# A hand-written issue order of 1,091 steps, listed anew, with one activation-table request ahead of the first logarithm

## The chip, the cores and the metric

The kernel runs on one NeuronCore of a Trainium2 chip. The core has five engines that work at the same time, each through its own instruction queue in order: TensorE (PE in the profile: matmuls; PEld: loads of the stationary operand), VectorE (DVE), ScalarE (ACT), GpSimd (POOL) and SyncE (SP, which here only issues DMAs). The metric is the device time of one execution in microseconds (us): the median of several runs.

## The reference, cut to what matters

```python
def _attn_ref(q, k, v, alpha):           # each (4, 8, 768, 48): batch, heads, tokens, head size
    state = zeros((B, H, 48, 48))
    for t in range(768):
        state = alpha[:, :, t, :, None] * state + einsum('bhd,bhe->bhde', k[:, :, t], v[:, :, t])
        y[:, :, t] = einsum('bhd,bhde->bhe', q[:, :, t], state)
    return y

x = y.transpose(0, 2, 1, 3).reshape(3072, 384)
h = x @ w_in                              # (384, 2048)
r = maximum(h, 0.0)
out = (s * (r * r) + b) @ w_out           # (2048, 384); s, b single numbers
```

A gated linear recurrence over 768 tokens gives 3072 rows of 384 numbers, which go through a two-layer network with a squared ReLU. Inputs and output are 32-bit floats.

## The kernel before, in words

**Blocks.** The 3072 rows are cut into 24 blocks of 128 rows, numbered n (or g) from 0 to 23; six blocks make one batch entry, and the state starts anew at blocks 0, 6, 12 and 18. Blocks 0 to 5, called windowed, are handled in pairs: an even block holds heads 0 to 3 and the following odd one heads 4 to 7 of the same 256 tokens.

**The recurrence of a block**, by the names of the steps and with the engine of each:

- `ln n` (ScalarE, L214): logarithm of alpha into la. `cum n` (TensorE, L225, L228, L239): running sums of it by matmuls with a triangle of ones, into the accumulator bank ct_ps.
- `ex n` (ScalarE, L249, L250, L253): exponentials of the sums and of their negatives, bi and b. For a windowed block a third gives the decay of the block (blast). For other blocks `decay n` (SyncE, L263, L265) writes the last row of b to DRAM and reads it back transposed, in three DMAs.
- `km n` and `qm n` (VectorE, L271, L279): k times bi, q times b. `tr n 1` and `tr n 0` (TensorE, L292): their transposes, again into ct_ps. `cp n` (VectorE, L299): copy of both out of ct_ps.
- `amat n` (TensorE, L320): products of k and q, into the two a_ps banks. `am n` (VectorE, L325): two masked copies out of them.
- `vcast n` (GpSimd, L219): v to 16 bits.
- `yi n` (TensorE, L340): the part of y from the state of the block before. `ya n` (TensorE, L356, L366): the part from within the block.
- `sp n` (TensorE, L382, L391): the block's addition to the state. `t1 n` (VectorE, L434, L436): new state. `sd n` and `sc n` (GpSimd, L444, L450): the state times the decay, for the next block's yi and t1.
- `yev n` (ScalarE, L400), `xt n` (TensorE, L408), `xev n` (ScalarE, L420): y out of its bank, transposed, and to 16 bits: the input of the network.

**The network of a block**, in four quarters u: `mp g u` (TensorE, L475, 12 matmuls of 128x128) into one of two banks h_ps in turn, `rl g u` (ScalarE, L489) the ReLU, `sq g u` (VectorE, L496) the square, `o g u` (TensorE, L511, 4 matmuls with 384 columns) into o_ps, and `oev g` out of it: by ScalarE (L524) for the first 13 blocks, which are kept and get their bias later (`add_bias`, VectorE, L563), by VectorE with the bias (L528) for the others. `store n` (SyncE) writes the rows. The last block's output is done in two halves of the columns (L539, L548).

**Setup.** `load_w` loads a pair of windowed blocks, whole or four heads at a time, `load` one block, `load_w_in i` and `load_w_out j0 j1` quarters of the weights (768 KB each). `win i kk` casts a piece of w_in to 16 bits (`a`: ScalarE, L619, `v`: VectorE, L621), `wout` a piece of w_out times s (VectorE, L171, or ScalarE, L179). `spread` (TensorE, L199, then VectorE) brings s and b to all partitions. `colsum`, `bias_sum` (VectorE, L186 to L191) and `bias_row` (TensorE, L195) form the bias row. `zero`, `ones`, `upper`, `eye` and `masks` fill constants on VectorE and GpSimd. `busy 1` is a matmul of 128x512 (L204) whose result nobody reads: filler work on TensorE; there are 37 of them. `table` (L569) requests, on ScalarE, the activation table that holds both logarithm and exponential; where an activation is met whose function is not in the table loaded last, the compiler puts a load of another table ahead of it.

**What sets the order.** No scheduler reorders anything. The string `order` (L629) lists 1,091 steps; the loop at L711 calls them one after the other, and each appends its instructions to the queues of its engines. So the list is, engine by engine, the order of each queue; waits between engines are put in from the data each step reads and writes. SyncE's queue is in list order too: a DMA whose buffer is not yet free, or a decay row not yet computed, holds every later DMA. DMAs take eight completion counters in turn, and one more is issued only when the eighth before it has landed.

## Time and profile before

| | |
|---|---|
| median of 3 runs | 199.38 us (199.14 to 199.48) |
| the profiled execution | 198.8 us, of which the profile's span is 197.0 us |
| TensorE busy | 186.6 us, 95% of the span |
| VectorE busy | 147.7 us, 75% |
| ScalarE busy | 119.6 us, 61% |
| GpSimd busy | 67.1 us, 34% |
| DMA | 30.34 MB moved; share of the 16 DMA engines about 1.0 up to 47 us, 0.55 from 47 to 191 us |
| first matmul, first `mp`, last matmul group | 1.94 us, 22.78 us, 191.16 us |

The span is one profiled execution on the chip, from its first to its last instruction. Busy time of TensorE counts a matmul until its modelled end, and matmuls overlap: the mean duration of an `mp` matmul is 219 ns, while one starts every 56 ns. To see a delay of TensorE, one compares the starts of successive matmuls. A row of the timeline gives start, duration, engine, line of the kernel, operation, result and operands, shape, and in brackets the idle time of the engine ahead of it with what ended it. A row of the waits gives who waited, for whom, the total, how often, and the longest.

### The profile page before, as it was taken

What the parts mean: (1) busy time and instruction counts of PE and PEld (TensorE: products, weight loads), DVE (VectorE), ACT (ScalarE), POOL (GpSimd) and SP (SyncE); (2) the same over time, 40 slices, a digit from 0 to 9 for tenths busy, and PEclk for the clock granted to TensorE, in tenths of its full rate; (3) what the DMA queues carried; (4) which work ended last, traced back from release to release, by engine and by line L of the source; (5) the groups of instructions that cost most, each with busy time, mean ns of one, the idle gap of its engine ahead of it and who ended that gap; (6) DMA issues with size and microseconds to landing.
All of it is one profiled execution on the core that took longest, in us unless ns stands there. A gap on an engine that the chain in (4) does not pass through costs nothing.

```text
span 197.0 us, 6345 instructions
## 1 busy us (share of the span) xinstructions
PE 186.6 (95%) x2593; PEld 146.6 (74%) x2595; DVE 147.7 (75%) x303; ACT 119.6 (61%) x246; POOL 67.1 (34%) x98
## 2 busy tenths in 40 slices
PE   4898999999999999999899899999999999999993
PEld 1466789757798877887577787887887778788873
DVE  5457897888689799588458476878988898885551
ACT  3825778934677849585437667657567465673530
...
GB/s 152 313 342 364 322 373 352 195 187 209 87 4 2 162 219 28 122 173 153 1 149 141 115 43 164 1 10 178 138 172 112 138 91 176 6 230 134 203 120 80
DMA packets 101119, 30.34 MB, mean 154 GB/s; under 512 B 94291, under 2 KB 99554, under 8 KB 101090
## 3 DMA queue, kind: packets, MB, share of 16 engines
...
q8 instruction: 20, 0.33, 0.7%
...
## 4 chain that ended last, share of the span: by engine, by line
PE 79%; DVE 8%; POOL 3%; ACT 3%; DMA 3%; issue 2%; POOLq 0%; ACTq 0%; DVEq 0%
PE h_ps L475 29%; PE o_ps L511 25%; PE ct_ps L292 5%; PE a_ps L320 4%; DMA a_sb<-in_alpha_dram 3%; PE o_ps L204 3%; POOL sd_sb L444 3%; DVE gt_all L496 2%; PE y_ps L366 2%; PE h_ps L408 2%; PE a_ps L539 1%; PE y_ps L340 1%; PE ct_ps L225 1%; PE p_ps L391 1%; DVE kb_sb L271 1%
## 5 line engine op out<-in xcount | busy, mean ns | idle before, releaser
L489 ACT ACTIVATE r_sb<-h_ps 128x512 bf16<-128x512 f32 x94 | 55.6, 599 | 33.7 <-PE h_ps L475 28.8
L475 PE MATMUL h_ps<-xd_all,w_in_bf 128*128 128x128 bf16 x1128 | 75.0, 219 | 0.0
L475 PEld LDWEIGHTS <-w_in_bf 128*128 128x128 bf16 x1152 | 67.7, 98 | 4.2
L511 PE MATMUL o_ps<-w_out_bf,gt_all 128*128 128x384 bf16 x336 | 64.7, 326 | 0.0
L444 POOL TENSOR_TENSOR sd_sb<-t_sb,blast_all 48x192 bf16<-48x192 f32 x40 | 29.3, 732 | 72.4 <-DVE t_sb L436 34.9
L511 PEld LDWEIGHTS <-gt_all 128*128 128x128 bf16 x368 | 32.8, 98 | 17.0 <-DVE gt_all L496 0.9
L496 DVE TENSOR_TENSOR gt_all<-r_sb 128x512 bf16<-128x512 bf16 x96 | 41.4, 456 | 5.2 <-ACT r_sb L489 5.2
L450 POOL TENSOR_TENSOR sc_sb<-t_sb,blast_all 112x384 f32<-112x384 f32 x16 | 17.6, 1100 | 29.0 <-DVE t_sb L436 15.9
L299 DVE COPY qkT<-ct_ps 112x1024 bf16<-112x1024 bf16 x24 | 16.5, 687 | 12.2 <-PE ct_ps L292 9.5
L219 POOL CAST v_bf<-v_sb 128x384 bf16<-128x384 f32 x24 | 17.6, 752 | 12.5 <-DMA v_sb<-in_v_dram 10.0
L271 DVE TENSOR_TENSOR kb_sb<-k_sb,bi_sb 128x384 bf16<-128x384 f32 x24 | 14.4, 600 | 7.3 <-ACT bi_sb L249 7.3
L249 ACT ACTIVATE bi_sb<-ct_ps 128x384 f32<-128x384 f32 x24 | 11.8, 490 | 12.3 <-PE ct_ps L225 6.2
L279 DVE TENSOR_TENSOR qb_sb<-q_sb,b_sb 128x384 bf16<-128x384 f32 x24 | 14.2, 591 | 5.0 <-ACT b_sb L250 4.9
L325 DVE TENSOR_TENSOR am_a<-a_ps,mask 128x512 bf16<-128x512 f32 x18 | 12.3, 684 | 5.6 <-PE a_ps L320 5.6
L420 ACT ACTIVATE xd_all<-h_ps 128x384 bf16<-128x384 bf16 x24 | 11.8, 490 | 5.4 <-PE h_ps L408 5.2
L400 ACT ACTIVATE y_bf<-y_ps 128x384 bf16<-128x384 f32 x21 | 10.4, 493 | 6.7 <-PE y_ps L366 5.5
L204 PE MATMUL o_ps<-mask,U_bf 128*128 128x512 bf16 x35 | 11.5, 456 | 2.3 <-DVE mask L600 1.9
L214 ACT ACTIVATE la_sb<-a_sb 128x384 bf16<-128x384 f32 x24 | 12.4, 519 | 0.0
L325 DVE TENSOR_TENSOR am_b<-a_ps,mask 128x512 bf16<-128x512 f32 x18 | 12.2, 678 | 0.0
L250 ACT ACTIVATE b_sb<-ct_ps 128x384 f32<-128x384 f32 x24 | 11.8, 492 | 0.0
L292 PE MATMUL ct_ps<-ident,kb_sb 128*112 128x128 bf16 x96 | 9.8, 225 | 0.8 <-DVE kb_sb L271 0.8
L292 PE MATMUL ct_ps<-ident,qb_sb 128*112 128x128 bf16 x96 | 9.8, 225 | 0.1
...
## 6 DMA issues: line engine op xcount, KB each, us to landing
...
```

The lines of the kernel that those rows point to most:

```text
L204: nc.tensor.matmul(out=o_ps, lhsT=U_bf, rhs=mask4.rearrange("a p t -> a (p t)"), start=True, stop=True,)
L219: nc.gpsimd.tensor_copy(out=by_head(v_bf[n % 3], n), in_=by_token(rows("v", n), n))
L271: nc.vector.tensor_tensor(out=by_head(kb_sb[n % 3][:, :, 0:48], n), in0=by_token(rows("k", n), n), in1=by_head(bi_sb[n % 2], n), op=ALU.mult,)
L292: nc.tensor.transpose(out=o, in_=t.rearrange("a h d -> a (h d)")[:, 128 * p : 128 * p + 112], identity=ident,)
L299: nc.vector.tensor_copy(out=qkT_sb[n % 2][0:112].rearrange("a x p t -> a (x p t)"), in_=t_ps[0:112].rearrange("a x p t -> a (x p t)"),)
L325: nc.vector.tensor_tensor(out=am_sb[e][n % 2], in0=a_ps[e], in1=m, op=ALU.mult)
L444: nc.gpsimd.tensor_tensor(out=sd_sb[n % 2][r, :, d], in0=t1_sb[r, :, d], in1=bl[r].to_broadcast([48, NP, 48]), op=ALU.mult)
L450: nc.gpsimd.tensor_tensor(out=sc_sb[0:112], in0=t1_sb[0:112], in1=blast[n % 4][0:112].to_broadcast([112, NP, 96]), op=ALU.mult,)
L475: nc.tensor.matmul(out=hp[:, jj * N : (jj + 1) * N], lhsT=w_in_bf[:, kk, 128 * j : 128 * (j + 1)], rhs=xd_sb[g][:, kk, 0:N], start=(kk == ...
L489: nc.scalar.activation(out=rs, in_=h_of.pop((g, u)), func=AF.Relu)
L496: nc.vector.tensor_tensor(out=gt_sb[g][:, u * 512 : (u + 1) * 512], in0=rs, in1=rs, op=ALU.mult)
L511: nc.tensor.matmul(out=op[:, 0:d_model], lhsT=gt_sb[g][:, j * C : (j + 1) * C], rhs=w_out_bf[:, j, :], start=(j == 0), stop=(j == NJ - 1),)
```

## The change

Both kernels call the same steps with the same arguments, only in another order; two things belong to it.

- `table` stands ahead of `ln 1; ln 0`, the first two logarithms. Before, it stood behind `ex 0`. The first logarithm is now ln 1, then ln 0.
- All of the list is written anew: filler matmuls, constants, loads, casts and the steps of the blocks stand in other places. For instance `spread` comes behind `tr 0 0`, `zero sd` and `win 2 2 v` come between `am 0` and `cp 1`, the first network quarter is `mp 0 0` instead of `mp 0 1`, `colsum 1` and `colsum 2` come behind `qm 5`, and `vcast 11` comes ahead of `sd 10`.

The diff, cut to the beginning of both lists and to the places that the prediction speaks of:

```diff
-        zero blast; zero ones_g; load_w a 0 0 4; upper n; load_w a 0 4 8; load_w k 0 0 4; zero kb; masks n; busy 1; ones g;
-        load_w q 0 0 4; load_w a 1; zero qb; busy 1; zero la; load_w q 0 4 8; busy 1; upper w; busy 1; zero sd; busy 1;
-        load_w k 0 4 8; load_w q 1; scalars; ln 0; load_w v 0; ln 1; cum 0; load_w_in 1; ex 0; table; busy 1; eye; ones f;
-        busy 1; busy 1; km 0; qm 0; tr 0 1; tr 0 0; masks w; busy 1; busy 1; busy 1; cp 0; cum 1; ex 1; load_w k 1; busy 1;
-        amat 0; busy 1; busy 1; km 1; busy 1; load_w_in 2; qm 1; busy 1; busy 1; ln 2; vcast 0; load_w_in 0; busy 1; am 0;
-        tr 1 1; tr 1 0; busy 1; busy 1; busy 1; cp 1; busy 1; spread; amat 1; am 1; cum 2; ex 2; busy 1; busy 1; busy 1;
-        ya 0; vcast 1; load_w v 1; sp 0; sp 1; ya 1; busy 1; busy 1; busy 1; busy 1; busy 1; win 1 0 a; yev 0; xt 0;
-        load_w a 2; ln 3; qm 2; xev 0; t1 0; km 2; tr 2 1; tr 2 0; load_w_in 3; sd 0; win 1 1 v; yi 1; win 1 2 v; busy 1;
-        cp 2; busy 1; load_w k 2; busy 1; busy 1; sc 0; win 2 1 v; yev 1; win 2 2 v; t1 1; win 2 0 a; busy 1;
-        load_w_out 0 4; win 0 2 v; cum 3; busy 1; busy 1; xt 1; ex 3; vcast 2; xev 1; km 3; amat 2; win 0 1 v; qm 3; am 2;
-        win 0 0 a; mp 0 1; load_w q 2; mp 1 2; rl 0 1; rl 1 2; load_w_out 4 8; tr 3 1; tr 3 0; mp 0 0; rl 0 0; sc 1; sd 1;
...
-        wout 2 4 0; sq 2 0; rl 2 1; t1 3; wout 0 2 1; mp 0 3; yi 3; yev 3; load_w v 2; mp 2 2; sc 3; load k 6; sq 1 3;
-        mp 2 3; o 2 0; rl 2 2; qm 4; tr 4 0; cp 4; wout 4 8 0; o 1 0; sq 1 1; xt 3; rl 0 3; sq 0 3; colsum 1; o 0 0; sq 2 1;
-        rl 2 3; ln 5; xev 3; wout 12 16 0; load a 6; cum 5; sq 2 3; mp 3 0; sq 2 2; o 0 1; wout 8 12 1; o 1 1; colsum 2;
-        o 2 1; o 1 2; load k 7; o 1 3; ex 5; oev 1; vcast 5; load a 7; rl 3 0; o 2 2; load q 6; o 2 3; km 5; tr 5 1; qm 5;
...
-        mp 5 3; t1 6; sp 7; load a 11; am 7; qm 8; tr 8 0; rl 5 3; sq 4 2; mp 6 2; ln 10; km 8; tr 8 1; vcast 8; mp 6 3;
...
-        ln 14; sq 9 2; rl 10 1; load v 13; sd 10; yi 11; vcast 11; ya 11; yev 11; rl 10 0; o 8 0; cum 13; o 8 1; amat 12;
...
-        mp 12 0; sp 14; load v 16; t1 14; rl 12 0; cum 15; sq 11 2; bias_row 1; ex 15; qm 15; amat 14; mp 12 3; rl 12 3;
...
+        zero la; zero ones_g; load_w a 0 0 4; zero qb; upper n; masks n; load_w a 0 4 8; busy 1; busy 1; eye; busy 1;
+        load_w k 0 0 4; upper w; busy 1; scalars; ones f; load_w q 0 0 4; table; busy 1; busy 1; ln 1; ln 0; zero blast;
+        ones g; zero kb; cum 0; busy 1; busy 1; ex 0; km 0; busy 1; tr 0 1; qm 0; tr 0 0; spread; busy 1; busy 1; busy 1;
+        load_w v 0; busy 1; load_w k 0 4 8; cp 0; load_w q 1; vcast 0; load_w q 0 4 8; load_w_in 2; load_w a 1; cum 1; ex 1;
+        masks w; km 1; load_w v 1; busy 1; busy 1; amat 0; busy 1; busy 1; busy 1; busy 1; win 2 0 a; qm 1; tr 1 1; tr 1 0;
+        am 0; load_w k 1; load_w_in 0; busy 1; busy 1; win 2 2 v; ln 2; busy 1; busy 1; ya 0; busy 1; zero sd; busy 1;
+        busy 1; cp 1; amat 1; am 1; cum 2; ex 2; busy 1; busy 1; busy 1; ln 3; busy 1; load_w_in 1; load_w_in 3; km 2;
+        vcast 1; sp 0; vcast 2; ya 1; yev 0; sp 1; t1 0; sd 0; xt 0; xev 0; win 0 2 v; qm 2; tr 2 1; tr 2 0; busy 1; yi 1;
+        yev 1; win 1 0 a; load_w a 2; busy 1; win 0 1 v; load_w q 2; busy 1; load_w_out 0 4; load_w_out 8 12; cp 2; sc 0;
+        cum 3; busy 1; busy 1; busy 1; win 0 0 a; mp 0 0; win 2 1 v; win 1 2 v; win 1 1 v; t1 1; ex 3; amat 2; qm 3; xt 1;
+        rl 0 0; mp 0 1; xev 1; km 3; tr 3 1; tr 3 0; rl 0 1; mp 0 2; win 3 0 v; mp 1 2; rl 0 2; rl 1 2; am 2; ln 4;
+        wout 0 2 1; sc 1; cp 3; load_w_out 4 8; sd 1; win 3 2 v; load_w k 2; sq 0 2; amat 3; mp 1 1; ya 2; win 3 1 v;
+        load_w_out 12 16; am 3; busy 1; rl 1 1; sq 1 1; yi 2; vcast 3; mp 1 0; sp 2; rl 1 0; ya 3; yev 2; wout 2 4 0; sp 3;
+        load a 6; t1 2; mp 1 3; rl 1 3; sd 2; load_w v 2; sq 1 0; xt 2; xev 2; load v 9; cum 4; o 1 0; sq 0 1; mp 2 0;
+        mp 2 2; mp 2 1; wout 4 8 0; sq 0 0; ex 4; km 4; rl 2 0; sq 1 3; ln 5; wout 8 12 1; rl 2 2; qm 4; o 1 1; sq 1 2;
+        load v 7; mp 0 3; rl 2 1; yi 3; load q 8; tr 4 1; tr 4 0; yev 3; mp 2 3; load q 6; rl 2 3; xt 3; o 1 2; load a 7;
+        xev 3; sc 2; load k 7; cp 4; cum 5; vcast 5; sq 2 1; mp 3 1; rl 0 3; t1 3; load k 6; sq 2 0; mp 3 0; o 2 0; o 2 1;
+        wout 12 16 0; vcast 4; ex 5; km 5; o 1 3; sq 2 2; o 2 2; tr 5 1; ln 6; sq 0 3; sq 2 3; rl 3 1; qm 5; colsum 1;
+        colsum 2; load a 8; rl 3 0; sd 3; sq 3 0; o 2 3; oev 1; o 0 0; tr 5 0; cp 5; oev 2; load v 6; load v 8; amat 4;
+        mp 3 2; rl 3 2; o 0 1; am 4; mp 3 3; rl 3 3; amat 5; cum 6; ln 7; ln 8; ex 6; o 0 2; o 0 3; sq 3 1; am 5; sp 4;
+        ya 4; oev 0; sq 3 3; sp 5; yi 4; load k 8; ya 5; sc 3; load a 9; o 3 0; load q 7; yev 4; t1 4; km 6; xt 4; o 3 1;
+        sd 4; yi 5; qm 6; xev 4; tr 6 0; tr 6 1; mp 4 0; yev 5; rl 4 0; colsum 3; cp 6; vcast 6; xt 5; sp 6; xev 5; cum 7;
+        amat 6; ex 7; sq 3 2; mp 4 3; rl 4 3; mp 5 1; rl 5 1; o 3 2; load v 10; load q 9; mp 4 1; mp 4 2; am 6; ya 6; km 7;
+        qm 7; rl 4 1; t1 6; rl 4 2; tr 7 0; sq 4 1; tr 7 1; cp 7; mp 5 0; yev 6; vcast 8; sq 4 2; xt 6; rl 5 0; vcast 7;
+        sq 4 3; o 3 3; sq 5 1; load a 12; oev 3; load k 9; sq 4 0; mp 5 2; cum 8; amat 7; xev 6; mp 6 2; decay 6; sd 6;
+        ex 8; decay 7; o 4 0; o 4 1; km 8; rl 5 2; sc 6; qm 8; tr 8 0; tr 8 1; sp 7; mp 5 3; rl 6 2; mp 6 3; rl 5 3; am 7;
...
+        load q 12; tr 10 1; ln 11; sd 8; rl 8 3; decay 9; mp 8 0; sq 6 0; rl 7 2; decay 10; yi 9; am 9; ya 9; cp 10; cum 11;
...
+        xev 9; km 11; mp 9 2; oev 6; tr 11 1; cp 11; load k 13; mp 8 1; ln 12; sq 7 3; sp 10; am 10; rl 9 2; o 7 0; rl 8 1;
...
+        tr 12 0; tr 12 1; load a 17; vcast 11; o 8 0; rl 9 1; o 8 1; sq 9 2; yev 10; sq 8 2; am 11; xt 10; xev 10; colsum 6;
...
+        ya 11; o 9 1; o 9 2; am 12; tr 13 0; yev 11; xt 11; rl 10 1; mp 10 3; load v 14; km 13; colsum 7; tr 13 1; cp 13;
+        vcast 13; xev 11; rl 10 3; mp 11 1; load a 14; ln 14; rl 11 1; sq 11 1; sp 12; t1 12; bias_sum; o 9 3; load a 16;
...
+        ya 14; mp 13 0; o 11 2; qm 15; sq 11 3; rl 12 2; yev 14; xt 14; rl 13 0; ln 16; sp 14; load v 18; sc 13; t1 14;
...
+        ln 18; load k 18; yi 15; sq 13 3; bias_row 1; km 16; vcast 15; qm 16; sp 15; add_bias 7; t1 15; ya 15; yev 15;
...
```

## The prediction

> **What bounds the kernel now.** I read the page's engine line first, then TensorE's list of waits, the timeline of the first 18 us, and the places in the timeline where TensorE starts late.
>
> The engine line says TensorE is the limit:
>
> ```profile
> PE 186.6 (95%) x2593; PEld 146.6 (74%) x2595; DVE 147.7 (75%) x303; ACT 119.6 (61%) x246; POOL 67.1 (34%) x98
> ```
>
> The work of the two kernels is the same, 37 fills included, so only TensorE's waits and the speed of its clock can move the end. The waits (what waited, for whom: us, times, longest):
>
> ```profile
> PE o_ps L204 <- DVE mask L600: 1.9, 1, 1.9
> PE p_ps L340 <- POOL sd_sb L444: 1.2, 2, 0.8
> PE ct_ps L228 <- ACT la_sb L214: 1.0, 1, 1.0
> PE y_ps L366 <- POOL v_bf L219: 1.0, 1, 1.0
> PE ct_ps L292 <- DVE kb_sb L271: 0.8, 3, 0.4
> PE p_ps L195 <- DVE t_sb L436: 0.5, 1, 0.5
> ```
>
> These count from the modelled end of a matmul; from start to start each is about 0.17 longer. The beginning, from the timeline (start, duration, engine, line):
>
> ```profile
> 3.33 1.28 ACT L214 ACT_TABLE_LOAD   x1 [3.33 <-DMA a_sb<-in_alpha_dram]
> 4.63 0.94 ACT L214 ACTIVATE la_sb<-a_sb 128x384 bf16<-128x384 f32 x2
> 5.58 1.28 ACT L249 ACT_TABLE_LOAD   x1
> 6.88 0.49 ACT L249 ACTIVATE bi_sb<-ct_ps 128x384 f32<-128x384 f32 x1
> 7.40 0.56 DVE L271 TENSOR_TENSOR kb_sb<-k_sb,bi_sb 128x384 bf16<-128x384 f32 x1 [3.63 <-ACT bi_sb L249]
> 8.95 1.49 PE L204 MATMUL o_ps<-mask,U_bf 128*128 128x512 bf16 x3
> 12.08 1.24 PE L204 MATMUL o_ps<-mask,U_bf 128*128 128x512 bf16 x5 [0.16 <-issue]
> 14.04 0.68 DVE L299 COPY qkT<-ct_ps 112x1024 bf16<-112x1024 bf16 x1
> ```
>
> Two table loads stand on the path: one begins only when alpha has landed, one delays the first exponential. Three fills take 1.49 us at 8.95 and five take 1.24 at 12.08: start to start 0.427 us each, later 0.216. TensorE is at half speed until about 11.1, though the granted-clock column reads 1.00 throughout. Later waits:
>
> ```profile
> 43.28 0.43 PE L292 MATMUL ct_ps<-ident,kb_sb 128*112 128x128 bf16 x4 [0.17 <-DVE kb_sb L271]
> 70.10 0.43 PE L292 MATMUL ct_ps<-ident,kb_sb 128*112 128x128 bf16 x4 [0.20 <-DVE kb_sb L271]
> 89.87 3.21 POOL L444 TENSOR_TENSOR sd_sb<-t_sb,blast_all 48x192 bf16<-48x192 f32 x2 [7.25 <-DMA a_sb<-in_alpha_dram]
> 93.14 0.33 PE L340 MATMUL y_ps<-sd_sb,qkT 112*128 112x96 bf16 x4 [0.19 <-POOL sd_sb L444]
> 93.15 2.58 POOL L219 CAST v_bf<-v_sb 128x384 bf16<-128x384 f32 x4
> 94.42 0.18 PE L366 MATMUL y_ps<-v_bf,am_a 128*128 128x48 bf16 x1 [0.96 <-POOL v_bf L219]
> 112.36 0.49 PE L195 MATMUL p_ps<-cs_sb,ones_f 128*128 128x128 f32 x2 [0.54 <-DVE t_sb L436]
> ```
>
> The rest is dense. From 113 to 190 no wait of TensorE over 0.2 us is shown.
>
> **The table request.** The built instruction lists show one table load on ScalarE instead of three, ahead of ln 1. The third load of before, 7.83 to 9.11, lay in ScalarE's idle time (next needed at 11.37), so it is worth nothing.
> The first load: the request waits for no data; ScalarE's two small DMA issues end at 1.50, so it runs from 1.5 to 2.8. But the list now has ln 1 before ln 0, and ln 1 reads the second alpha transfer, whose completion the trace has at 4.20 (the first at 3.26). ln 1 runs at 4.24, ln 0 at 4.67 (0.43 apart in before) and ends at 5.18. cum 0, which reads ln 0, starts at 5.23 against 5.20. Worth nothing; what is late next is the alpha transfer.
> The second load: cum 0's last matmul ends at 6.31, so ex 0 starts at 6.34 instead of 6.88: 0.54 earlier, and tr 0 at 7.48 instead of 8.01.
> [...]
>
> **The new list, beginning.** The mask copy moves behind the zeroing of la and qb (0.55 each) instead of kb (0.82): it ends at 2.22, not 1.89, and the first fill starts 0.33 later. Six fills at 0.427 then end at 4.83, still ahead of 5.23, so it costs nothing. Between cum 0 and cum 1 seven fills stand instead of six, and spread (0.31) comes forward: tr 0 ends 8.42, spread 8.72, four fills at 0.427, cum 1 at 10.43 against 10.23. The 0.54 is used up. ex 1 at 11.48 (11.37).
> VectorE's order then matters: km 1 12.0, qm 1, am 0 (two of 0.60) to 14.1, and now a cast of w_in (0.41) and the zeroing of sd (0.43) ahead of cp 1. cp 1 starts at 14.9 against 14.04, amat 1 at 15.65 against 14.87. 26 fills are done by then instead of 22, so some of this is work done ahead. Next cum 2, ex 2, am 1, sp 1, t1 0, and sd 0 on GpSimd, as slow as at 18.01 (1.92 the pair): yi 1 at 20.75 against 19.98.
> SyncE's queue is saturated to 47 us (DMA share about 1.0), so I place each load by summed kilobytes at the landings of before: w_in 2 (2688 KB) 12.1, a 1 13.4, k 1 16.0, w_in 0 18.1, w_in 1 20.3, all in time. w_out rows 4-8 (9216 KB) land at 32.3 and k 2 at 33.4; o 1 1, listed 5.3 us of TensorE work earlier than before, needs that cast (1.05): 33.4. Carrying this on to cum 5, where both lists have issued 27.3 us of TensorE work: 37.5 against 36.90. Cost 0.6.
>
> **The new list, middle.** For each later wait I sum the TensorE work listed between the matmul that starts a chain and the one that ends it, less the chain's rows (ex 0.55, VectorE items in order, 0.06 for a semaphore):
> km 5, qm 5 before tr 5 (waits at 43.3 and 43.8): short by 0.7 and 1.05 in before, room 2.0 and 1.7 in after, because the two colsums (1.06 each) stand behind. With an output group that ran 0.31 late at 41.6, this is 0.31 + 0.34 + 0.20 = 0.85 from start to start. Goes.
> km 8 and qm 8 (70.1): short 0.4 and 0.3, now room 1.4 and 0.6. 0.36 goes.
> yi 11 and ya 11 (93.1, 94.4): the cast of v 11 was listed behind sd 10 and with no work ahead of ya 11; now ahead of sd 10 with 6.2 us. 0.35 + 1.12 goes.
> bias_row 1 (112.4) follows sp 14 by 0.26 us of work, now 4.8. 0.71 goes.
> yi 5 after sd 4 (52.1): work between 1.9, now 1.8; the wait stays.
> Sum of these after 47 us: 2.54; I count 2.2, since something later is usually late next. New: oev 0 ahead of o 3 0 has ScalarE items ln 7, ln 8, ex 6 in front: short 0.4. Cost 0.4. All other places past 47 us have room above -0.25 on VectorE and ScalarE and above 0.6 on GpSimd.
> The decay DMAs keep their pairs and stand behind two more loads (at about 51 instead of 49.3): the first, for sd 6, has over 6 us left. The loads behind decay 10 (k 13, v 11, a 13 to a 14) leave at about 1 us each from about 78 and are needed from 92 on. Nothing.
> The tail has the same pieces (2.65 of matmul, an addition, a store). Nothing.
>
> **Sum.** +0.6 - 0.85 - 2.2 + 0.4 = -2.05. The profiled execution took 198.8 (span 197.0 and 1.8 around it); the median of three is 199.38, 0.6 above it. I subtract from the median: 197.3.
>
> **Rivals.**
> *The clock comes up earlier.* In before TensorE idled 1.0 before cum 0 and 0.4 before tr 0; in after it works almost without a gap from 2.3. If full speed came at 7.7 instead of 11.1, cum 1 would start at 9.8 (cp 0's end), ex 1 at 10.5, amat 1 at 14.7, yi 1 at 19.85; w_out's landing at 32.3 holds cum 5 to 37.2, or 36.9 if it lands sooner. 0.3 to 0.6 less: 196.8. Against: one trace, one turning point. Chance 0.15.
> [...]
> *Other waits take the place.* Each item that now comes in time uncovers the next, and TensorE has no slack to absorb an irregular GpSimd span (1.08 to 3.21 for the sd pair). Then -0.2 is left: 199.2. For: VectorE 75% busy. Against: the tally's rooms are mostly above 0.6. Chance 0.15.
> *Slower: VectorE's queue between km 1 and the first output groups.* The list has 10.4 us of VectorE work on 8 us of TensorE work (between 16 and 24 us of it; before 8.0), and from am 1 to o 1 0 the room is -2.06 (before +2.5). With GpSimd running, squares took 1.05 instead of 0.41 (31.65) and two casts 0.97 instead of 0.74 (20.92). Eight items stretched by 0.3 are 2.4 us more; TensorE waits for them at amat 3, ya 3 or o 1 0. Beyond 2.05 more than I walked it decides; at 2.9 the time is 200.2. Chance 0.20.
>
> **How the numbers follow.** Forecast 0.50, its own range 196.4 to 198.6. 0.2% (0.40 us) is about what a measurement tells from no change. Faster: 0.48 + 0.15 + 0.05 = 0.68; same: 0.02 + 0.09 + 0.01 = 0.12; slower 0.20. The range goes from 195.9 (all of 2.54, no new wait, early clock) to 199.9 (most of the slower case), leaving out about 0.15.
>
> **What would show it.** One table load ending near 2.8, ln 1 first at 4.2; ex 0 near 6.3; amat 1 near 15.6 (14.7 with an early clock); cum 5 near 37.5; no wait for v_bf, kb_sb (L292) or t_sb (L195) past 40; yi 5 still waiting. I am wrong if TensorE idles over 1 us between 12 and 36, or if a late load holds a cast.

## The result

The changed kernel takes 202.88 us (median of 20 executions, 199.97 to 204.5) against 199.53 of the kernel before (20 executions, 198.02 to 199.9): 1.0138 times as long, 95% interval 1.0110 to 1.0167. It is about 1.4% slower; I had forecast 197.3. The profiled execution took 202.97, with a span of 201.2. A ratio, here and below, sets a kernel's executions within 1.5% of its fastest (11 of these 20) against those of the kernel before run beside them, so it is not the quotient of the medians shown; one execution of 648 us, of swap_v1_later, is left out.

The work is as before; TensorE has become a smaller share of a longer span. The page's engine line, and its row of the granted clock (tenths of full speed, 40 slices of 5 us):

```profile
PE 187.5 (93%) x2591; PEld 147.2 (73%) x2595; DVE 150.5 (75%) x303; ACT 116.9 (58%) x244; POOL 65.9 (33%) x98
PEclk9999699999999999999999999999999999999999
```

The 6 in the fifth slice is new: TensorE's granted clock was at 1.00 and was taken back to 0.50, from 20.90 to 24.31 us. Its list of waits (who waited, for whom: us, times, longest):

```profile
PE ct_ps L292 <- DVE qb_sb L279: 2.7, 2, 2.3
PE o_ps L204 <- DVE mask L600: 2.2, 1, 2.2
PE p_ps L340 <- POOL sd_sb L444: 1.3, 1, 1.3
PE p_ps L391 <- ACT bias_w L196: 0.8, 1, 0.8
```

The waits for v_bf, for t_sb ahead of the bias row and for kb_sb past 40 us are gone. One of 2.3 us has come, for a `qm`; sd 4 (yi 5) and the bias row wait longer or anew.

**Where the time went.** I take the start of a matmul and subtract what TensorE's own matmuls so far cost at full pace (start to start 0.056 each for `mp`, 0.162 for `o`, and so on, 163.8 in all) and 37 fills at 0.216. What is left is lost: idle, half speed, and the small regular gaps.

| | before | changed | difference |
|---|---|---|---|
| lost up to 36 us | 10.1 | 14.0 | +3.8 |
| 36 to 60 us | 2.7 | 2.8 | +0.1 |
| 60 us to the last matmul | 9.1 | 8.2 | -1.0 |
| from the last matmul's start to the end | 3.3 | 4.5 | +1.2 |

The sum is +4.2, the difference of the two spans.

**The beginning.** Rows that answer to those of before (start, duration, engine, line): one table load, then the logarithms, the first exponential, the first transpose.

```profile
1.53 1.28 ACT L569 ACT_TABLE_LOAD   x1 [1.53 <-PEq L729]
4.50 0.94 ACT L214 ACTIVATE la_sb<-a_sb 128x384 bf16<-128x384 f32 x2 [1.69 <-DMA a_sb<-in_alpha_dram]
6.61 0.49 ACT L249 ACTIVATE bi_sb<-ct_ps 128x384 f32<-128x384 f32 x1 [1.17 <-PE ct_ps L239]
7.74 0.68 PE L292 MATMUL ct_ps<-ident,kb_sb 128*112 128x128 bf16 x4
```

From there to 18 us the walk of the prediction holds within 0.4 us. Then this, in the same view (SyncE's issues, two VectorE rows, TensorE):

```profile
9.78 2.80 SPq L147 DMA_DIRECT2D k_sb<-in_k_dram  x1
12.62 2.21 SPq L153 DMA_DIRECT2D w_in_st<-in_moe_w_in_dram  x3
...
19.81 0.47 DVE L621 CAST w_in_bf<-w_in_st 128x512 bf16<-128x512 f32 x1 [1.04 <-DMA w_in_st<-in_moe_w_in_dram]
20.20 1.17 DVE L279 TENSOR_TENSOR qb_sb<-q_sb,b_sb 128x384 bf16<-128x384 f32 x1
...
21.43 0.68 PE L292 MATMUL ct_ps<-ident,qb_sb 128*112 128x128 bf16 x4 [2.28 <-DVE qb_sb L279]
```

The issue of k 1 holds SyncE's queue for 2.80, so w_in 0 is issued at 12.62; it lands at 19.78. `win 0 2 v` waits for it, idle 1.04, and behind it in VectorE's queue stands `qm 2`, whose data had come. `qm 2` then takes 1.17, where `qm 1` took 0.55 at 12.54 (GpSimd's sc 0 runs beside it, from 20.07 to 20.96). TensorE stands still for 2.3.

The DMA engines are behind by then as well. The windows view for the first 18.1 us, where the prediction has w_in 0 landed, of the kernel before and then of the changed one (the last number is GB/s): 5.25 MB have been moved against 4.83.

```profile
0.00:18.10 18.10, 14.45 (x149) 8.48 (x152) 10.79 (x35) 9.19 (x18) 4.14 (x21) 1.00 0.95 290
0.00:18.10 18.10, 15.10 (x150) 8.32 (x152) 10.11 (x34) 6.65 (x16) 4.53 (x21) 1.00 0.92 267
```

The same view (busy us of TensorE first, after the stretch; the granted clock third from the end) shows what follows: in the first stretch TensorE was busy for 1.25 of 3.41 us, in the second it has half speed.

```profile
17.49:20.90 3.41, 1.25 (x40) 0.96 (x39) 2.00 (x4) 1.52 (x5) 1.83 (x3) 1.00 1.01 356
20.90:24.31 3.41, 2.66 (x17) 1.98 (x18) 2.32 (x6) 1.42 (x3) 0.06 (x1) 0.50 1.08 336
```

**The middle.** Two waits took the place of those that went, yi 5 on sd 4 and sp 15 on the copy of the bias row out of their common bank (p_ps), here in the timeline:

```profile
53.05 2.59 POOL L444 TENSOR_TENSOR sd_sb<-t_sb,blast_all 48x192 bf16<-48x192 f32 x2 [9.06 <-DVE t_sb L436]
55.70 0.33 PE L340 MATMUL p_ps<-sd_sb,qkT 112*128 112x96 bf16 x4 [1.30 <-POOL sd_sb L444]
...
125.84 0.38 ACT L196 ACTIVATE bias_w<-p_ps,sb_col 128x128 f32<-128x128 f32 x1
126.28 0.34 PE L391 MATMUL p_ps<-v_bf,kb_sb 128*128 128x96 bf16 x4 [0.78 <-ACT bias_w L196]
```

**The tail.** SyncE issues without a pause from 189.63; six issues for windowed rows and one more stand ahead of store 22 (197.49) and of the last block's two halves (197.97 on), whose last addition began at 196.97:

```profile
193.08 3.68 SPq L558 DMA_DIRECT2D out_dram<-w_in_st  x6
196.81 0.58 SPq L555 DMA_DIRECT2D out_dram<-w_in_st  x1
197.49 0.39 SPq L555 DMA_DIRECT2D out_dram<-out_sb  x1
197.97 0.90 SPq L549 DMA_DIRECT2D out_dram<-out_sb  x2
```

In the kernel before, SyncE was idle ahead of the last block's two halves, whose last addition began at 194.00:

```profile
191.94 0.34 SPq L555 DMA_DIRECT2D out_dram<-out_sb  x1
193.72 0.99 SPq L549 DMA_DIRECT2D out_dram<-out_sb  x2
```

### The profile page after: what moved, and what is told of

Same layout as the page of the kernel before. It is cut to its first block, busy times and chain, and to the rows that moved or that the text cites. A ratio compares the mean times of both kernels' runs of the same rounds, so it can differ in the third digit from the quotient of the medians.

```text
span 201.2 us, 6335 instructions
## 1 busy us (share of the span) xinstructions
PE 187.5 (93%) x2591; PEld 147.2 (73%) x2595; DVE 150.5 (75%) x303; ACT 116.9 (58%) x244; POOL 65.9 (33%) x98
## 4 chain that ended last, share of the span: by engine, by line
PE 74%; DVE 8%; SPq 6%; DMA 5%; issue 3%; ACT 2%; POOL 0%; ACTq 0%; DVEq 0%
PE h_ps L475 27%; PE o_ps L511 24%; SPq L147 5%; PE ct_ps L292 4%; DMA w_in_st<-in_moe_w_in_dram 4%; PE a_ps L320 3%; PE a_ps L511 3%; DMA k_sb<-in_k_dram 2%; DVE qb_sb L279 2%; PE ct_ps L225 2%; PE h_ps L408 2%; PE y_ps L366 2%; PE a_ps L539 1%; PE p_ps L391 1%; DVE gt_all L496 1%
## 5 line engine op out<-in xcount | busy, mean ns | idle before, releaser
L511 PE MATMUL o_ps<-w_out_bf,gt_all 128*128 128x384 bf16 x336 | 63.8, 326 | 0.0
L444 POOL TENSOR_TENSOR sd_sb<-t_sb,blast_all 48x192 bf16<-48x192 f32 x40 | 29.9, 747 | 92.2 <-DVE t_sb L436 56.1
L496 DVE TENSOR_TENSOR gt_all<-r_sb 128x512 bf16<-128x512 bf16 x96 | 42.3, 462 | 10.2 <-ACT r_sb L489 10.0
L450 POOL TENSOR_TENSOR sc_sb<-t_sb,blast_all 112x384 f32<-112x384 f32 x16 | 16.9, 1059 | 12.6 <-DVE t_sb L436 11.7
L271 DVE TENSOR_TENSOR kb_sb<-k_sb,bi_sb 128x384 bf16<-128x384 f32 x24 | 16.6, 691 | 5.7 <-ACT bi_sb L249 5.7
L219 POOL CAST v_bf<-v_sb 128x384 bf16<-128x384 f32 x24 | 16.5, 706 | 12.9 <-DMA v_sb<-in_v_dram 12.4
L249 ACT ACTIVATE bi_sb<-ct_ps 128x384 f32<-128x384 f32 x24 | 11.8, 490 | 9.6 <-PE ct_ps L239 7.6
L279 DVE TENSOR_TENSOR qb_sb<-q_sb,b_sb 128x384 bf16<-128x384 f32 x24 | 15.9, 662 | 1.7 <-ACT b_sb L250 1.6
L420 ACT ACTIVATE xd_all<-h_ps 128x384 bf16<-128x384 bf16 x24 | 11.8, 493 | 8.3 <-PE h_ps L408 8.2
L204 PE MATMUL o_ps<-mask,U_bf 128*128 128x512 bf16 x33 | 12.0, 485 | 2.6 <-DVE mask L600 2.2
L400 ACT ACTIVATE y_bf<-y_ps 128x384 bf16<-128x384 f32 x21 | 10.3, 490 | 4.9 <-PE y_ps L366 4.4
L250 ACT ACTIVATE b_sb<-ct_ps 128x384 f32<-128x384 f32 x24 | 11.8, 492 | 0.0
L292 PEld LDWEIGHTS <-qb_sb 128*112 128x112 bf16 x96 | 8.2, 136 | 3.9 <-DVE qb_sb L279 3.0
```

Source lines behind the costliest of these rows:

```text
L219: nc.gpsimd.tensor_copy(out=by_head(v_bf[n % 3], n), in_=by_token(rows("v", n), n))
L271: nc.vector.tensor_tensor(out=by_head(kb_sb[n % 3][:, :, 0:48], n), in0=by_token(rows("k", n), n), in1=by_head(bi_sb[n % 2], n), op=ALU.mult,)
L279: nc.vector.tensor_tensor(out=by_head(qb_sb[n % 2][:, :, 0:48], n), in0=by_token(rows("q", n), n), in1=by_head(b_sb[n % 2], n), op=ALU.mult,)
L292: nc.tensor.transpose(out=o, in_=t.rearrange("a h d -> a (h d)")[:, 128 * p : 128 * p + 112], identity=ident,)
L444: nc.gpsimd.tensor_tensor(out=sd_sb[n % 2][r, :, d], in0=t1_sb[r, :, d], in1=bl[r].to_broadcast([48, NP, 48]), op=ALU.mult)
L450: nc.gpsimd.tensor_tensor(out=sc_sb[0:112], in0=t1_sb[0:112], in1=blast[n % 4][0:112].to_broadcast([112, NP, 96]), op=ALU.mult,)
```

## The experiments

Theory after the two traces: a cast that waits for a late load stands ahead of the blocks' own steps (2.3), the clock is taken back for it (about 1.2), and the last stores queue (1.2). Rivals: VectorE is behind in the beginning wherever the cast stands; the landings hold the first network quarters themselves; the table part does harm.

All results, with the lost time as above (from one profiled execution each):

| kernel | median us (n) | ratio to before, 95% | lost to 36 us | 36 us to last matmul | behind it |
|---|---|---|---|---|---|
| before | 199.53 (20) | 1 | 10.1 | 11.8 | 3.3 |
| changed | 202.88 (20) | 1.0138 [1.0110, 1.0167] | 14.0 | 11.0 | 4.5 |
| cast_behind | 202.32 (6) | 1.0144 [1.0102, 1.0186] | 13.4 | 11.1 | 4.0 |
| gap_fills | 201.68 (6) | 1.0140 [1.0107, 1.0172] | 13.2 | 11.1 | 3.8 |
| early_stores | 201.92 (5) | 1.0142 [1.0114, 1.0170] | 14.2 | 11.0 | 3.3 |
| colsum_later | 202.39 (1) | one execution | 14.3 | 10.3 | 4.3 |
| after_ln0 | 203.38 (6) | 1.0168 [1.0130, 1.0206] | 15.0 | 11.0 | 4.4 |
| casts_behind_chain | 201.88 (6) | 1.0123 [1.0098, 1.0148] | 13.2 | 11.4 | 4.1 |
| landing_order | 201.90 (12) | 1.0097 [1.0059, 1.0136] | 12.9 | 11.5 | 4.9 |
| swap_quarters | 202.29 (6) | 1.0131 [1.0098, 1.0165] | 11.6 | 11.4 | 4.2 |
| swap_v1_later, again | 201.22 (5), 201.89 (2) | 1.0102 [1.0073, 1.0131] | 13.0 | 11.4 | 4.5 |
| after_mended | 199.14 (12) | 0.9973 [0.9947, 0.9998] | 12.0 | 10.3 | 3.3 |
| mended_casts | 198.94 (12) | 0.9958 [0.9935, 0.9981] | 11.3 | 10.3 | 3.3 |
| mended_wout | 197.74 (12) | 0.9941 [0.9905, 0.9976] | 11.1 | 9.9 | 3.3 |
| table_alone | 198.40 (12) | 0.9942 [0.9914, 0.9970] | 10.1 | 11.9 | 3.3 |
| head_of_before | 197.88 (9) | 0.9903 [0.9868, 0.9938] | 9.1 | 11.2 | 3.3 |
| table_ln0 | 195.68 (4) | 0.9810 [0.9786, 0.9835] | 8.0 | 10.9 | 3.3 |
| ln0_local | 194.15 (6) | 0.9752 [0.9715, 0.9788] | 9.8 | 9.6 | 3.3 |
| best | 193.86 (5) | 0.9712 [0.9690, 0.9734] | 8.9 | 8.3 | 3.3 |

In gap_fills the ten more fills count as lost. The edits of the first nine kernels are small against the spread of the executions, so what each does is read from its trace. A traced execution can lie off the median: that of swap_quarters (200.73) is 1.6 below it, that of ln0_local (196.28) 2.1 above.

### The parts of the change, apart

```diff
 table_alone (from the kernel before)
-scalars; ln 0; load_w v 0; ln 1; cum 0; load_w_in 1; ex 0; table;
+scalars; table; ln 1; ln 0; load_w v 0; cum 0; load_w_in 1; ex 0;
```

> The kernel before with the first part of the change alone: the table request ahead of the first logarithm, and ln 1 ahead of ln 0. Theory A (my working of the table part: ex 0 0.54 earlier, tr 0 0.5 earlier, and TensorE's later work follows): 0.3 to 0.5 less than before, about 199.1. Rival B (cp 0 and cum 1 are reached earlier, but later steps of the beginning wait for loads and VectorE as before): within 0.2 of 199.5. Rival C (this part does harm, for instance by a cum 0 that now comes when TensorE has had fewer fills, so that full speed comes later): 0.4 or more above 199.5.

0.8 less than the kernel before run beside it (199.18; ratio 0.9942): the table part helps, by more than theory A allowed, and rivals B and C fall. The profiled execution, 198.89, shows nothing of it up to 36 us; four of the twelve took 196.8 to 197.1. Those have no trace, so why they are 1.5 faster stays open; an earlier rise of the clock is a candidate (last section).

```diff
 table_ln0 (from the kernel before)
-scalars; ln 0; load_w v 0; ln 1; cum 0; load_w_in 1; ex 0; table;
+scalars; table; ln 0; load_w v 0; ln 1; cum 0; load_w_in 1; ex 0;
```

> The kernel before with the table request ahead of the first logarithm and ln 0 still ahead of ln 1. ln 0 reads the first alpha transfer (landed 3.26 in the kernel before), so cum 0 can start near 3.9 instead of 5.2. Theory A (the first two table loads were both on the path, and the exchange of ln 0 and ln 1 is what made the first one worth nothing): ex 0 near 5.1, km 0 as soon as k lands (5.4 to 5.7), tr 0 near 6.3 to 6.7, so that TensorE's idle ahead of cum 0 shrinks by about 0.8 and full speed comes in the first window more often; 0.3 to 0.8 less than with ln 1 first (198.4), about 197.8. Rival (the later steps of the beginning wait for k 1 and the casts all the same): within 0.3 of 198.4.

The largest result of the study: 195.68, 2.7 below the same list with ln 1 first. Timeline, logarithms and cum 0:

```profile
3.54 1.11 ACT L214 ACTIVATE la_sb<-a_sb 128x384 bf16<-128x384 f32 x2 [0.72 <-DMA a_sb<-in_alpha_dram]
4.12 0.64 PE L228 MATMUL ct_ps<-la_sb,Ui_bf 128*128 128x192 bf16 x3
```

cum 0 starts at 4.12 instead of 5.20 in the kernel before. Both of its first table loads were on the path; the exchange of the logarithms is what made the first one worth nothing. TensorE has lost 8.0 up to 36 us against 10.1. The 2.7 is over three times what theory A allowed, and not all of it is the earlier chain: in this trace TensorE is at full speed by 5.0 us (that it gets there by windows, as the expectation has it, was an assumption), and the last section shows what that alone is worth in this list.

```diff
 after_ln0 (from the changed kernel)
-ln 1; ln 0;
+ln 0; ln 1;
```

> The changed kernel with ln 0 ahead of ln 1, nothing else. With the kernel before this exchange, beside the early request, was worth 2.7 (198.4 with ln 1 first, 195.7 with ln 0 first). Theory A (the same holds in the new list: cum 0 starts near 4.1 instead of 5.2, the chain of the beginning and the clock come earlier and the whole list follows): 2.0 to 2.7 below 202.9, about 200.5. Theory B (the head of the new list is bound by the landings of w_in and by VectorE from 15 us on, so an earlier start is given back there): cum 0 near 4.1 all the same, but the losses of TensorE up to 36 us stay within 1 of those of the changed kernel with an early clock, and the time is 201.5 to 202.9.

Theory B. cum 0 starts 0.8 earlier (4.69 against 5.49), and the cast waits the longer:

```profile
20.85 0.43 DVE L621 CAST w_in_bf<-w_in_st 128x512 bf16<-128x512 f32 x1 [2.52 <-DMA w_in_st<-in_moe_w_in_dram]
...
21.80 0.67 PE L292 MATMUL ct_ps<-ident,qb_sb 128*112 128x128 bf16 x4 [3.45 <-DVE qb_sb L279]
```

The time, 203.38, is no shorter than that of the changed kernel, and 0.5 above theory B's range. So in the new list an earlier start is worth nothing: the beginning ends when w_in has landed, here at 20.83.

```diff
 head_of_before: steps 1 to 291 (to about 53 us) of table_alone, then the steps
 that are left in the order of the changed kernel, and in these
+store 1, 6, 11, 12 behind store 7;  bias_row 1 behind mp 14 0
```

> The first 291 steps (to about 53 us) in the order of the kernel before with the table request and ln 1 ahead of ln 0, the rest in the order of the changed kernel, with store 1, 6, 11 and 12 moved up and bias_row 1 moved up behind mp 14 0. Theory A (the head of the new list is what costs, its middle gains about 1.0 from 60 to 193 and would gain 1.9 without the wait of sp 15 for the bias row, its last stores cost 1.2): 1.9 less than the table alone (198.4), about 196.5. Rival (the gain of the middle comes only behind the late head, which gives VectorE and GpSimd a lead, or other waits take the place): 198.0 to 199.5.

The profiled span is 195.4, 1.7 below that of table_alone, but 1.0 of this lies up to 36 us, where both run the same steps; the medians differ by 0.5, and the executions spread from 196.4 to 199.8. The 1.9 of theory A is not borne out. The old beginning takes away the loss up to 36 us (9.1 against 14.0). At the seam yi 5 waits 1.80 (start to start). Shown is that the beginning is what costs; how much the rest of the new list gains is 0.7 by the lost time (11.9 to 11.2).

### The beginning: cast, clock or landing

```diff
 cast_behind
-xt 0; xev 0; win 0 2 v; qm 2; tr 2 1; tr 2 0; ... load_w a 2; busy 1; win 0 1 v; ... cp 2;
+xt 0; xev 0; qm 2; tr 2 1; tr 2 0; ... load_w a 2; busy 1; win 0 2 v; win 0 1 v; ... cp 2;
```

> The changed kernel with one step moved: the cast win 0 2 v, which reads w_in 0 (landed 19.78 in the trace of the changed kernel), stands behind yi 1 and yev 1 instead of ahead of qm 2. Theory A (the cast's wait holds qm 2, tr 2 0 and so TensorE for 2.3 us, and the half-speed stretch of 3.4 us behind it comes from that idle): qm 2 starts near 18.8 instead of 20.20, TensorE's wait for qm 2 falls from 2.3 to under 0.8, the clock stays at full speed between 20 and 30, and the time falls by 1.5 + 1.2 = 2.7, from 202.9 to about 200.2. Rival B (VectorE is too far behind in the beginning anyway; the cast only names the place): the wait comes back at cp 2 or amat 2, which now stand behind the cast; the time stays within 0.6 of 202.9. Rival C (the idle goes, the clock drops all the same): 1.5 less, 201.4, with half speed still granted for some us.

Rival B as far as the time goes. qm 2 is in time, and the wait comes back behind the cast, at cp 2 and so at cum 3; the clock is taken back there (22.1 to 25.5; the granted clock is 0.71 over 20 to 25 us and 0.95 over 25 to 30):

```profile
19.82 1.37 DVE L621 CAST w_in_bf<-w_in_st 128x512 bf16<-128x512 f32 x2 [1.09 <-DMA w_in_st<-in_moe_w_in_dram]
...
21.84 0.43 PE L228 MATMUL ct_ps<-la_sb,Ui_bf 128*128 128x192 bf16 x3 [1.36 <-DVE qkT L299]
```

```diff
 gap_fills
-tr 2 1; tr 2 0;
+tr 2 1; busy 1 (ten times); tr 2 0;
```

> The changed kernel with ten more filler matmuls (0.216 each, 2.16 together) between tr 2 1 and tr 2 0, where TensorE waits 2.3 us for qm 2. They move no other step; the wait for qm 2 itself stays. Theory A (the half-speed stretch behind the wait is a consequence of TensorE's idling and costs on its own): full speed stays granted from 20 to 30, tr 2 0 still starts at 21.4, and the time falls by 0.8 to 1.5 to about 201.7. Rival (the stretch of half speed is hidden behind the other engines, or is not brought about by the idling): the time stays within 0.4 of 202.9, or a half-speed stretch is still there.

Full speed stays, as the windows view has it for the stretch around the wait:

```profile
19.19:22.60 3.41, 2.65 (x19) 1.29 (x18) 1.87 (x4) 0.09 (x1) 1.51 (x3) 1.00 1.02 384
```

The lost time up to 36 us is 0.8 to 1.1 less than in the three traces of the same beginning with the clock taken back (changed kernel, early_stores, colsum_later), the median 1.2 less: the clock costs about 1.0 of the 3.8, and nothing where the wait is filled. The ratio does not resolve it.

```diff
 casts_behind_chain
-... am 0; ... win 2 2 v; ... zero sd; ... cp 1; amat 1; am 1; ... win 0 2 v; qm 2; ... win 0 1 v; ... cp 2;
+zero kb; zero sd; ... am 0; ... cp 1; amat 1; am 1; win 2 2 v; ... qm 2; ... cp 2; win 0 2 v; win 0 1 v;
```

> The changed kernel with VectorE's casts of w_in out of the way of the first blocks, no load moved: win 2 2 v behind am 1 instead of ahead of cp 1, win 0 2 v and win 0 1 v behind cp 2 instead of ahead of qm 2 and cp 2, and zero sd among the first zeroings. Theory A (what costs in the head is that casts which wait for a load stand in VectorE's queue ahead of cp 1, qm 2 and cp 2): the waits at amat 1, tr 2 0 and cum 3 shrink to under 0.6 each, the clock is not taken back, what TensorE does not spend on the kernel's own matmuls up to 36 us falls from 21.4 to 22.2 in the runs so far to about 19, and the time is about 200.3. Rival B (the landings themselves: the first mp needs the quarter that lands at 19.8 and the next one that of 22.3, so the wait moves to mp 0 0 and mp 0 1): 201.5 to 202.5, with a wait of over 1 at the first mp.

The waits at amat 1, qm 2 and cp 2 shrink (one of 1.0 is left at cum 2); one of 1.8 stands ahead of the first `mp`, and the clock is taken back behind it (that `mp` takes 1.22 us, one at 47.52 in the changed kernel 0.84; the mean granted clock of the span is 0.991). As rival B says, but not for its reason. Timeline of ScalarE and TensorE:

```profile
22.66 1.15 ACT L619 ACTIVATE w_in_bf<-w_in_st 128x512 bf16<-128x512 f32 x2 [2.02 <-DMA w_in_st<-in_moe_w_in_dram]
...
23.87 1.22 PE L475 MATMUL h_ps<-xd_all,w_in_bf 128*128 128x128 bf16 x12 [1.67 <-ACT w_in_bf L619]
```

ScalarE's first cast reads w_in 1 (22.64); the second, for the `mp`, reads w_in 0, which had landed at 20.44. The same pattern on another engine: a cast whose load is not there, ahead of one whose load is.

```diff
 landing_order (casts_behind_chain, and)
-win 1 0 a; ... win 0 0 a;        ln 4; wout 0 2 1; ... yev 2;
+win 0 0 a; win 1 0 a;            ln 4; ... yev 2; wout 0 2 1;
```

> The changed kernel with no load moved, its casts of w_in behind the blocks' own steps on VectorE as in casts_behind_chain (201.88), and two more casts put behind on ScalarE: win 1 0 a behind win 0 0 a, wout 0 2 1 behind yev 2. In casts_behind_chain ScalarE waited for w_in 1 (22.64) at win 1 0 a, with w_in 0 (20.44) landed, and TensorE waited 1.83 for win 0 0 a behind it, ahead of the first mp; its clock was then taken back for 3.4 us. Theory A (what holds the head are casts that stand in an engine's queue ahead of work whose data has come, not the landings): the wait ahead of the first mp falls under 0.5, full speed stays, and the time falls by 1.5 to 2.0, to about 200.1. Rival (the landings: mp 0 1 needs w_in 1, so the wait moves there): within 0.6 of 201.9, a wait of over 1 at the second mp.

The wait ahead of the first `mp` is 0.2, and none over 0.75 is left between 12 and 36 us; yet the lost time is 12.9, the clock is taken back once more (0.985 on the mean of the span), and the median stays at 201.9. Seven waits of 0.45 to 0.75 are left, at cum 2, xt 0, km 2 (which waits for k 1), qm 2, sd 0, cum 3 and cp 3; five of these places waited in casts_behind_chain too. Moving casts without moving loads wins little: theory A falls by the median, and the rival's wait at the second `mp` did not come either. The traced execution, 202.86, is one of the longer of the twelve; two took 199.5 and 200.1, near theory A's 200.1, and have no trace.

```diff
 swap_quarters
-load_w_in 2 (first of w_in), load_w_in 0 (second); win 2 0 a, win 2 2 v first; win 0 2 v ahead of qm 2
+load_w_in 0 first, load_w_in 2 second; win 0 0 a, win 0 2 v first; win 0 1 v ahead of qm 2; win 2 2 v behind mp 0 0
```

> The changed kernel with the loads of the quarters 0 and 2 of w_in exchanged, and their casts with them; the last cast of quarter 2 stands behind mp 0 0, so that nothing ahead of cp 2 reads the load that lands near 19.8. The quarter of the first mp is then the one that lands near 12.7. Theory A (the head of the changed kernel is held by w_in 0 landing at 19.78, wherever its casts stand: with the cast moved, cp 2 and cum 3 waited instead of qm 2): no wait of TensorE over 1 us between 17 and 25, the first mp starts at about 22.5 to 23.5 instead of about 25, the clock is not taken back, and the time is 2.0 to 3.0 below 202.9, about 200.3. Rival B (VectorE's order and its backlog in the beginning hold TensorE): at most 0.8 less, 202.2, with new waits for cp 1, km 2 or cp 2. Rival C (all loads of the first 25 us are late by 1 to 1.7 in the new order, and the next one holds TensorE in its turn): a wait at amat 2, mp 0 1 or mp 0 2 takes the place, 201.5 to 202.5.

The quarter of the first `mp` now lands at 12.4. TensorE has no wait over 1 us up to 36 and lost 2.4 less there; the profiled execution is the shortest of the six, and the median gains only 0.6: by the median rival B, and only this trace goes the way of theory A.

```diff
 swap_v1_later (swap_quarters, and)
-load_w v 1; load_w k 1; load_w_in 2; load_w_in 1;     vcast 2; ... sc 0;
+load_w k 1; load_w_in 2; load_w_in 1; load_w v 1;     sc 0; vcast 2;
```

> The kernel with quarters 0 and 2 of w_in exchanged (202.3), and load_w v 1 (384 KB, first read by vcast 2) moved from ahead of k 1 to behind load_w_in 1, with vcast 2 behind sc 0. Theory A (the late landings of the second and third quarter of w_in, 19.0 and 21.4, hold the casts and, through the casts that pile up on VectorE behind them, t1 1, km 3, am 2 and cp 3): both land about 1.1 earlier, the waits at amat 2, the first mp and amat 3 (0.81, 0.71, 0.61 start to start) shrink together by 1.0 or more, the time is near 201.2. Rival (VectorE's order itself is what holds these steps, whenever the weights come): the landings move, the waits stay within 0.4, 202.0 to 202.4.

> The kernel with quarters 0 and 2 of w_in exchanged and v 1 loaded later, once more, for a profiled execution that can be read: the earlier one was disturbed (648 us). Theory A: the second and third quarter of w_in land near 17.9 and 20.3 instead of 18.97 and 21.40, the waits at amat 2, the first mp and amat 3 (0.81, 0.71, 0.61 with v 1 early) are together smaller by 1.0, near 201.2. Rival: the landings move, the waits stay.

The second and third quarter land at 18.0 and 20.1, and the three waits are 1.5 less together (0.81, 0.71 and 0.61 became none, 0.23 and 0.38; the one that I called the first `mp` is at mp 0 1). A new one of 1.35 comes at 31.9, for a ReLU. The median of the five executions is 1.1 below swap_quarters, as theory A said, though the ratios (1.0102 and 1.0131) do not resolve it; the trace, from the second run, had its first full speed as late as 11.6.

### All places put right

```diff
 after_mended (swap_v1_later, and)
+ln 0 ahead of ln 1;  store 1, 6, 11, 12 behind store 7;  colsum 3 behind cp 6;  bias_row 1 behind mp 14 0
 mended_casts (after_mended, and)
+zero sd behind zero kb;  win 0 2 v behind am 1;  win 0 1 v behind cp 2
 mended_wout (mended_casts, and)
+wout 0 2 1 behind yev 2
```

> The changed kernel with all that was found put right: ln 0 first, quarters 0 and 2 of w_in exchanged, v 1 loaded later, store 1, 6, 11 and 12 earlier, colsum 3 behind cp 6, bias_row 1 behind mp 14 0. Theory A (each of these places cost on its own: exchange of the logarithms 2.0 to 2.7, head 1.5, stores 1.1, yi 5 0.9, bias row 0.9): 202.9 less 6.4 to 7.1, about 196.2. Rival (behind each stands the next wait): half of it, about 199.5.

> The kernel with all places put right (199.14), with its casts out of the way as well: win 0 2 v behind am 1, win 2 2 v is behind mp 0 0 already, zero sd among the first zeroings. Theory A (the wait of 1.33 at amat 1 is the cast of quarter 0, landing 13.8, ahead of cp 1): the wait falls under 0.4 and the time by about 1.0, to 198.1. Rival (the steps behind wait for k 1 and for the second quarter in its place): within 0.3 of 199.1.

> The kernel with all places put right and the casts of w_in out of the way (198.94), with one more cast moved: wout 0 2 1 (ScalarE, reads w_out rows 0 to 3, landed 28.73) behind yev 2 instead of ahead of rl 1 1. In that kernel ScalarE was idle for 2.46 ahead of this cast and TensorE waited 1.40 (start to start) at 30.22 for the ReLU behind it. Theory A (the third place of the same kind: a cast on a late load, ahead of a block's own step): the wait at 30.22 falls under 0.4, the time by 1.0 to 1.4, to about 197.7. Rival (o 1 0, which reads this cast, waits in its place): within 0.3 of 198.9.

199.14: 3.7 less than the changed kernel, about half of what I had added up. mended_casts takes the wait of 1.33 at amat 1 away, and one of 0.68 for a ReLU grows to 1.40, at 30.22, for 0.2 in the end. (It moves win 0 1 v too, which its expectation does not name.) There the pattern shows a third time: ScalarE waits for w_out at a cast, and the ReLU behind it is late:

```profile
28.75 0.93 ACT L179 ACTIVATE w_out_bf<-w_out_st,sb_col 128x768 bf16<-128x768 f32 x1 [2.46 <-DMA w_out_st<-in_moe_w_out_dram]
...
30.22 0.83 PE L475 MATMUL h_ps<-xd_all,w_in_bf 128*128 128x128 bf16 x12 [1.22 <-ACT r_sb L489]
```

With that cast behind yev 2 the wait is gone. The median is 197.74, 1.2 less, as theory A said, but the two lost times differ by 0.6 together and the ratios (0.9941 and 0.9958) by less still, so the size is not shown. Still 11.1 are lost up to 36 us, where the old list with ln 0 first loses 8.0 to 9.8. That rest is spread over waits of 0.2 to 1.0 and was not taken apart further: it stays open.

### The middle and the tail

```diff
 early_stores
-store 6; ... store 12; store 11; ... store 1;   (in the last 10 us)
+store 7; store 6; store 12; store 11; store 1;  (some 20 us earlier)
```

> The changed kernel with store 1, 6, 11 and 12 moved up behind store 7 (listed some 20 us before the end), nothing else. Theory A (SyncE's issues of the last stores hold the last store back: in the changed kernel 4.26 us lie between TensorE's end and the end of the span, 3.04 in the kernel before): the stretch behind TensorE falls to about 3.0 to 3.2 and the time by 1.1, to 201.8. Rival (the last landing takes what it takes; the queue is not what holds it): 202.9, the stretch stays at 4.2.

The stretch from the last matmul's start to the end is 3.3, as in the kernel before, instead of 4.5. Its last rows of SyncE's queue:

```profile
195.89 0.59 SPq L555 DMA_DIRECT2D out_dram<-w_in_st  x1
196.58 0.39 SPq L555 DMA_DIRECT2D out_dram<-out_sb  x1
197.07 0.89 SPq L549 DMA_DIRECT2D out_dram<-out_sb  x2
```

Theory A by the trace (the median is 1.0 less; the ratio does not resolve it).

```diff
 colsum_later
-rl 4 0; colsum 3; cp 6;
+rl 4 0; cp 6; colsum 3;
```

> The changed kernel with colsum 3 (VectorE, 0.95) behind cp 6 instead of ahead of it, so that VectorE is idle in the second half of sd 4. Theory A (the pair of GpSimd multiplications of sd takes 2.59 at 53.05 because VectorE works beside it without a pause; with VectorE pausing it took 1.59 in the kernel before): the pair takes under 2.1 and TensorE's wait at yi 5 falls from 1.46 (start to start) to under 1.0. Rival (the duration of GpSimd's multiplications does not depend on VectorE): 2.5 to 2.6, the wait stays at 1.4 to 1.5.

Theory A: 1.73 instead of 2.59, and yi 5 waits 0.59 (start to start) instead of 1.46.

```profile
53.58 1.73 POOL L444 TENSOR_TENSOR sd_sb<-t_sb,blast_all 48x192 bf16<-48x192 f32 x2 [8.57 <-DVE t_sb L436]
...
55.36 0.33 PE L340 MATMUL p_ps<-sd_sb,qkT 112*128 112x96 bf16 x4 [0.43 <-POOL sd_sb L444]
```

```diff
 ln0_local (table_ln0, and)
+vcast 11 behind tr 12 0;  bias_row 1 behind mp 13 0;  yi 5, yev 5 behind ln 7, mp 4 0;  km 8 ahead of sq 4 2
 best (ln0_local, and)
+colsum 1 and 2 behind qm 5;  o 8 0 ahead of yi 11
```

> The kernel before with the table request first and ln 0 still ahead of ln 1 (195.68), and four single moves against four waits of its middle, each as the new list has them: vcast 11 behind tr 12 0, bias_row 1 behind mp 13 0, yi 5 and yev 5 behind mp 4 0, km 8 ahead of sq 4 2. The waits are 1.12, 0.71, 0.60 and 0.36, together 2.8. Theory A (a wait of TensorE that is given room gives its time back, as I counted 2.2 of 2.54 for the middle of the new list): 2.2 to 2.8 less, about 193.2. Rival (others take the place, as in the changed kernel, where the middle gained about 1.0 of them): 1.0 less, 194.7.

> The kernel before with the early request, ln 0 first and the four moves of its middle (194.15), and two more: colsum 1 and 2 behind qm 5, o 8 0 ahead of yi 11. The waits aimed at are 0.31 + 0.34 + 0.20 between 41 and 44 and 0.36 at 92.5. Theory A (each gives its time back): 0.8 to 1.2 less, about 193.2. Rival (the next wait takes the place, as at yi 5, whose move gave 0.1 of 0.6): 193.9 to 194.2.

In ln0_local TensorE loses 2.1 less behind 60 us, of the 2.19 that three of the four waits make: a wait given room there gives its time back. The fourth, yi 5, gave 0.1 of its 0.6, since tr 7 then waited 0.46 for km 7. The medians differ by 1.5, between theory A and its rival. In `best` the waits at 41 to 44 and at 92.5 are gone and 1.3 less is lost behind 36 us; the median is 0.3 less, within the spread of the two kernels, as its rival said. What is left of TensorE's waits:

```profile
PE o_ps L204 <- DVE mask L600: 1.9, 1, 1.9
PE ct_ps L292 <- DVE kb_sb L271: 0.8, 3, 0.3
PE ct_ps L228 <- issue: 0.8, 1, 0.8
PE ct_ps L228 <- DVE qkT L299: 0.7, 2, 0.4
```

At 193.86 (0.9712) it beats both kernels.

## Why the prediction was wrong

**Table request: right.** One load ending at 2.81; ln 1 waits for the second alpha transfer; ex 0 at 6.61 (I said 6.34: alpha landed 0.3 later). That the first load is worth nothing because "the list now has ln 1 before ln 0" was right, and table_ln0 shows how much hung on that choice: 2.7, with the clock's part in it. "The 0.54 is used up" was too strict for the old list, where the part alone gives 0.8 in the medians.

**Beginning: +0.6, measured +3.8. This step failed.** cum 1 (10.85 against 10.43), ex 1 (11.54 against 11.48) and amat 1 (15.63 against 15.65) came as walked. The failing words are "w_in 0 18.1 ... all in time". By summed kilobytes at before's landings I had 18.1; it landed at 19.78 (18.97 to 20.83 in the other traces with v 1 loaded as early), and VectorE was at that cast at 18.77. So the term that was mis-sized is the landing, by 1.7: at 18.1 it would have been in time there too. The 0.42 MB that the changed kernel had moved less by 18.1 are 1.2 of it, at the 342 GB/s that it moved from 10 to 18.1 (an estimate); why it had moved less stays open. And the walk gives the cast no place in VectorE's queue, where `qm 2` stands behind it; there the late load became 2.3 us of TensorE, 0.6 of them `qm 2` itself, 1.17 long beside GpSimd; with the cast moved behind (cast_behind) 1.5 came at cum 3 instead. yi 1 came at 22.3 instead of 20.75, cum 5 at 40.88 instead of 37.5. Both things that I had named as proof against me came: TensorE idled over 1 us between 12 and 36, and a late load held a cast. Half speed was the second part, not foreseen: about 1.0. It came at 20.90, behind 3.41 us in which TensorE was busy for 1.25. I had reckoned with the clock for the gain alone.

**Middle: right in what goes, wrong in what comes.** The waits at 41 to 44 (0.85) and of 70.1, 93.1, 94.4 and 112.4 (2.54) are gone. For yi 5 "the wait stays" became 1.46 instead of 0.59: I had compared the work ahead of it (1.8 and 1.9) and not what VectorE does beside sd 4. The 0.4 at o 3 0 did not appear. Missed were sp 15 behind bias_row 1 (0.94), where the tally did not know that both use p_ps, and tr 9 on qm 9 and amat 9 on cp 9 (0.55, 0.26): km 9 and qm 9 take 0.85 and 1.18 at 71.98 and 72.75, with GpSimd at work beside them, against 0.55 each for km 7 and qm 7 (59.22, 59.69). Counted -2.65 with the wait at o 3 0, measured -0.9. ln0_local shows that the count itself, a wait given room gives its time, was sound.

**Tail: 0, measured +1.2.** "The same pieces" was true of the last additions and stores, and I did not look at what SyncE's queue holds ahead of them.

**Rivals.** That full speed comes at 7.7 was a supposition; in the changed kernel's own trace it came at 10.7. It did come earlier, at 5.0 to 5.8, in four traces with the new beginning (in cast_behind three fills take 0.81 at 5.66, in the changed kernel 1.44 at 6.43), and its gain was eaten by the same landing (in early_stores TensorE waited 2.96 from start to start, against 2.45). The slower rival had the right engine and stretch, VectorE's queue between km 1 and the first output groups, but for the most part another mechanism: instructions stretched beside GpSimd, where it was one instruction without its data (`qm 2` took 0.6 longer). Its 200.2 was 2.7 short.
